# The last query group in two parts, a seventh buffer of exponentials, clears on VectorE, and a later planned use of the broadcast reciprocals, in a fused attention and feed-forward kernel

## The chip, the cores and the metric

One Trainium2 chip (trn2), one core. The metric is the device time of one execution in microseconds; smaller is better. The **span** of a profile runs from the first to the last instruction and is some 1.7 us shorter. PE is TensorE, DVE is VectorE, ACT is ScalarE, POOL is GpSimd, SP is the queue that issues transfers.

## The reference, cut

```python
def reference(A_x, A_wqkv, A_wo, B_x, B_w1, B_w2, B_w3, B_w4):   # x: 1 x 2048 x 640, bf16
    def _A_ref(x, wqkv, wo):                                     # 32 heads of 20
        ...
        scores = jnp.einsum("bhqd,bhkd->bhqk", q, k) * (Dh ** -0.5)
        p = _softmax(scores, axis=-1)
        o = jnp.einsum("bhqk,bhkd->bhqd", p, v)
        return (...)(o, 0, 2, 1, 3).reshape(B, S, D) @ wo
    ...                                                          # _B_ref: two feed-forward blocks
    xn = _layernorm(x, axis=-1)
    s = _A_ref(xn, A_wqkv, A_wo)
    g = _silu(_B_ref(xn, B_w1, B_w2, B_w3, B_w4))
    ...                                                          # out = a product of s and g, plus x
```

The heart is 32 x 2048 x 2048 exponentials. Four heads ("a quad") and 512 queries make a **group**; there are 8 x 4 = 32 groups. A group has 16 key tiles of 128, and each key tile needs two exponentials of 128 x 1024 elements.

## The kernel before, the parts that matter

The program is a list of tasks. A planner in the kernel file gives every task a place in the order of its engine, from modelled durations and hand-tuned due times (`DUE`); a change of any number can move everything. The table `ND` says, for every quad and group, how many **units** DVE takes: a unit is one pair of key tiles, of which DVE computes half in place of ACT (by bit arithmetic, two reads of 128 x 1024 and four pieces), so a unit takes two exponentials off ACT.

```python
        self.POOLN = [1, 9, 13, 15]          # normalisations done by POOL
        self.ND = (
            [1, 2, 3, 3],                    # quad 0, its four groups
            ...
            [4, 3, 1, 2])                    # quad 7
...
            pl.pool("PT", 6)                 # buffers of exponentials
...
        T("pool", 3000, lambda e: e.memset(self.QM[:, :, :, :], 0.0), ..., name="qm0")
        T("pool", 1500, lambda e: e.memset(self.KT[:, 1, :], 0.0), ..., name="kt0")
        T("pool", 1500, lambda e: e.memset(self.QT[:, 1, :], 0.0), ..., name="qt0")
...
    # end of a group: sums to DRAM and back, reciprocals, broadcast by DMA, product
        T("sp", C_SP, lambda e: e.dma_start(RB[:, :], bass.AP(dr.tensor, ...)), ..., name=f"r1{quad}_{qc}", dlat=1100.0)
        T("dve", c_dve(512, "1x"), lambda e: e.tensor_tensor(dst, Ob[:, :], RB[:, :], op=ALU.mult),
          reads=[A("Ob"), A("RB")], writes=[dsta], name=f"on{quad}_{qc}")
...
    # last quad, after a group: output projection, gate, sum, store, for each of its 4 results
            else:
                for hh in range(2):
                    self.wo_mult("wob", n, hh, range(cfg.KC + 1), SB2[:, sl, :], A("SB2", sl, hh))
            T("dve", c_dve(cfg.D, "2x"), lambda e, ...: e.tensor_tensor(OS[:, sl, :], SB2[:, sl, :], addend, op=ALU.add), ..., name=f"cmb{n}")
            T("sp", C_SP, lambda e, sl=sl, n=n: e.dma_start(outv[:, n, :], OS[:, sl, :]), ...)
```

`wob` is the projection of attention's result (PE, twelve tasks of four matmuls of 320 columns per result); its eviction on DVE multiplies by the gate. There are 16 results of 128 rows; the last four can only be finished after the last exponential.

Of the kernel before, what the change touches and what calls it, by code (L numbers as in the profile page):

```python
# [610 lines left out]
class Cfg:  # L611
# [5 lines left out]
    def __init__(self, S=2048, D=640, H=32, F=1536):  # L617
        self.S, self.D, self.H, self.F = S, D, H, F
        self.DH = D // H
        assert self.DH == 20 and D % 128 == 0 and F % 128 == 0 and S % 512 == 0  # L620
        self.NT = S // 128
        self.NQC = S // 512
        self.KC = D // 128
        self.FC = F // 128
        self.NQUAD = H // 4
        self.QW = 4 * self.DH
        self.scale = self.DH ** -0.5
        self.OFFSET = 60.0
        self.T0 = 38000.0
        self.STEP = 960.0  # L630
        self.DUE = dict(
            k0=100.3, k1=-164.3, k2=-87.4, k3=-108.7, k4=-66.2, v0=-24.5, v0s=-0.38, v1=48.3, v1s=-24.33, w1=675.4,
            w1s=6.41, g1=135.1, x1=243.0, x1s=-5.42, wo=135.2, st=56.8, g3_0=400.7, g3_2=603.1, si_0=451.5, si_2=689.9,
            sis=9.71, u0=9.1, s0=-19.7, u1=5.8, s1=19.9, u2=-21.8, s2=-19.6, u3=-17.5, s3=-7.9, u4=-6.0, s4=-6.6,
            u5=-24.2, s5=8.6, u6=-28.0, s6=-9.3, u7=-1.9, s7=126.8)
        self.BLK = [(2, 3), (6, 7), (10, 11), (14, 15)]
        self.RESERVE = 1000.0
        self.POOLN = [1, 9, 13, 15]
        self.HPE = 0.0
        self.HDVE = 0.0  # L640
        self.THIRD = False
        self.FALL = True
        self.SAVE = 1
        self.AHEAD = 3
        self.UNITS = ((),
                      ((3, 0, 1),),
                      ((0, 0, 2), (2, 1, 2)),
                      ((0, 0, 2), (2, 1, 2), (7, 0, 1)),
                      ((0, 0, 2), (1, 1, 2), (3, 0, 2), (5, 1, 2)))
        self.HPS = 6  # L650
        self.FILL = 0
        self.ROWK = [[], [], [], [], []]
        self.ND = (
            [1, 2, 3, 3],
            [3, 3, 3, 4],
            [3, 3, 3, 3],
            [2, 3, 4, 4],
            [4, 2, 2, 4],
            [4, 3, 3, 3],
            [4, 4, 2, 3],  # L660
            [4, 3, 1, 2])

    def order(self, quad, qc):



        nb = self.ND[quad][qc]
        used = [k for b in self.BLK[:nb] for k in b]
        ks = [k for k in range(self.NT) if k not in used]
        at = {}  # L670
        for j, (pos, r, n) in enumerate(self.UNITS[nb]):
            at.setdefault(pos, []).append(("b", j, r, n))
        out = []
        for i in range(len(ks) + 1):
            out += at.pop(i, [])
            if i < len(ks):
                out.append(("k", ks[i], i in self.ROWK[nb]))
        assert not at
        return out
# [37 lines left out]
class Gen:  # L717
# [71 lines left out]
    def build(self, plan_only=False):  # L789
        nc, pl = self.nc, self.pl  # L790
        with contextlib.ExitStack() as es:
# [21 lines left out]
            pl.pool("PT", 6)  # L813
# [51 lines left out]
    def setup_consts(self):  # L865
# [34 lines left out]
        self.maskn6 = m6  # L900
        Mm = self.Mm = self.alloc("Mm", [2, 32], BF16)
        T("pool", 200, lambda e: e.memset(Mm[:, :, :], 0.0), writes=[A("Mm", 0), A("Mm", 1)], name="Mm0")

    def alloc_persistent(self):
# [19 lines left out]
        self.PT = self.alloc("PT", [6, 1024], BF16)  # L924
        self.QM = self.alloc("QM", [2, 4, 512], BF16)
        T("pool", 3000, lambda e: e.memset(self.QM[:, :, :, :], 0.0), writes=[A("QM", k) for k in range(2)], name="qm0")
# [23 lines left out]
        T("pool", 1500, lambda e: e.memset(self.KT[:, 1, :], 0.0), writes=[A("KT0")], name="kt0")  # L950
        T("pool", 1500, lambda e: e.memset(self.QT[:, 1, :], 0.0), writes=[A("QT0")], name="qt0")
# [16 lines left out]
    def ln_tiles(self, tag, tiles, dst_of, dst_atoms_of, ve_out=None):  # L968
# [27 lines left out]
        for li, n in enumerate(tiles):  # L996
            pool = ve_out and n in cfg.POOLN
            T("pool" if pool else "dve", 160 + 0.86 * D if pool else c_dve(D, "4x"),
# [5 lines left out]
    def ln_tiles_act(self, tag, tiles):  # L1004
# [10 lines left out]
        for li, n in enumerate(tiles):  # L1015
            T("act", c_act(D) + 135, lambda e, li=li, n=n: e.activation(J[:, :], xn[:, n, :], AF.Copy, accum_out=sv[:, 0, li:li + 1]),
              reads=[A("xn", n)], writes=[A(tag + "_J"), A(tag + "_sv", 0, li)], name=f"{tag}_sx{n}")
            T("act", c_act(D) + 135, lambda e, li=li, n=n: e.activation(J[:, :], xn[:, n, :], AF.Square, accum_out=sv[:, 1, li:li + 1]),
              reads=[A("xn", n)], writes=[A(tag + "_J"), A(tag + "_sv", 1, li)], name=f"{tag}_sxx{n}")
# [14 lines left out]
        for li, n in enumerate(tiles):  # L1034
            if n in self.cfg.POOLN:
                T("pool", 160 + 0.86 * D,
# [3 lines left out]
            T("act", c_act(D) + 40,  # L1040
# [25 lines left out]
    def ln1_and_transpose(self):  # L1066
# [5 lines left out]
        for g0 in range(0, NT, 8):  # L1072
            for k0, L in ((0, 2), (2, 2), (4, 1)):
                tl = list(range(g0 + k0, g0 + k0 + L))
                tmp += self.ln_tiles(f"ln1_{g0 + k0}", tl, lambda n: xn[:, n, :], lambda n: [A("xn", n)], ve_out=True)
            tmp += self.ln_tiles_act(f"ln1a_{g0}", list(range(g0 + 5, g0 + 8)))
        self.ln1_tmp = tmp
        bk = 0
        for g in range(4):
            for kc in range(cfg.KC):  # L1080
                b = bk % 4
                act = bk % 2 == 1
# [187 lines left out]
    def v_proj(self, hf):  # L1270
# [8 lines left out]
        T("pool", c_pool(cfg.NT * 16), lambda e: e.memset(VA[:, :, :, :, 20:21], 1.0), writes=allv, name=f"VA1_{hf}")  # L1279
        T("pool", c_pool(cfg.NT * 16), lambda e: e.memset(VA[:, :, :, :, 21:22], 0.0), writes=allv, name=f"VA0_{hf}")  # L1280
# [18 lines left out]
    def attn_quad(self, quad):  # L1299
# [9 lines left out]
        for qc in range(NQC):  # L1309
# [3 lines left out]
            if col:  # L1313
# [3 lines left out]
                  stream="qm", ndma=4)  # L1317
            done, total = [0], sum(5 if x[0] == "b" else 1 for x in seq)
# [3 lines left out]
            for kind, x, *unit in seq:  # L1322
                if kind == "k":
                    if col and unit[0]:
                        heads = (0, 2, 1, 3)
                        slots = [self.score_half(b, qc, x, a, gb) for a in range(2)]
                    else:
                        heads = range(4)
                        slots = [self.score_act(b, qc, x, a, gb if col else None) for a in range(2)]
                    kts = (x, x)  # L1330
                else:
# [4 lines left out]
                    heads = range(4)  # L1336
# [4 lines left out]
                def fnpv(e, kts=kts, slots=slots, ends=ends, heads=heads):  # L1341
                    pb = self.bank(PVB)
                    first, final = ends()
                    for x, i in enumerate(heads):
                        ins = e.matmul(pb[32 * i:32 * i + 22, 0:512], VA[:, ql, kts[x // 2], i, :],  # L1345
                                       PT[:, slots[x // 2][0].slot, 512 * (x % 2):512 * (x % 2) + 512],
# [5 lines left out]
            if last:  # L1352
                self.finish_qc(qc)
                if qc == 0:
                    self.part_qc(NQC - 1)

# [33 lines left out]

    def score_half(self, b, qc, kt, a, gb):

        T, A = self.T, self.A
        hs, sa = self.stile()
        def fn(e):
            for jj in range(2):
                r = slice(64 * jj, 64 * jj + 64)
                ins = e.matmul(self.bank(hs.slot + jj)[:, :], self.KT[r, b, 128 * kt:128 * kt + 128], self.QM[r, gb, a + 2 * jj, :],
                               start=True, stop=True, tile_position=(64 * jj, 0))
            return ins  # L1400
        T("pe", 220, fn, reads=self.turns() + [("gate",), A("KT", b, kt // 4), A("QM", gb)],
          writes=[sa, ("turn", self.step)], name=f"sc{self.step}", mode=1, cls=-1, acq=("S", hs))
        return self.exp_act(hs, sa)
# [74 lines left out]
    def normalise(self, quad, qc):  # L1478
# [7 lines left out]
        if last:  # L1486
            dst, dsta = self.On7[:, 512 * qc:512 * qc + 512], A("On7", qc)
        else:
            dst, dsta = self.On[:, ob, :], A("On", ob)
        if last:  # L1490
            OnT = self.On[:, ob, :]
            cls = -2 if qc == cfg.NQC - 1 else -1
# [10 lines left out]
            T("dve", c_dve(512, "1x"), lambda e: e.transpose(dst, OnT[:, :]), reads=[A("On", ob)], writes=[dsta], name=f"on{quad}_{qc}", cls=cls)  # L1503
# [14 lines left out]
          reads=[("dr", ob)], writes=[A("RB")], is_dma=True, nbytes=128 * 2048, name=f"r1{quad}_{qc}", stream="r1", dlat=1100.0)  # L1518
        T("dve", c_dve(512, "1x"), lambda e: e.tensor_tensor(dst, Ob[:, :], RB[:, :], op=ALU.mult),  # L1519
          reads=[A("Ob"), A("RB")], writes=[dsta], name=f"on{quad}_{qc}")  # L1520
# [7 lines left out]
    def load_wo(self):  # L1528
# [7 lines left out]
        T("pool", 1500, lambda e: e.memset(OTq[:, :, KC - 1, :], 0.0), writes=[A("OTq", k) for k in range(2)], name="otq0")  # L1536
        self.Sb = self.alloc("Sb", [4, D], BF16)
# [10 lines left out]
    def wo_tile(self, name, n, hh, parts, dst_atoms, first_reads=()):  # L1548
# [13 lines left out]
        def rd(k):  # L1562
            return [A("OTq", o), A("Wo")] if ps[k] < KC else [A("On7", n // 4), A("Wo7")]
# [29 lines left out]
    def wo_last(self, n, dst, dsta):  # L1593
# [11 lines left out]
        T("pe", c_pe(8, HALF), fn, reads=[A("On7", n // 4), A("Wo7")], writes=[sa], name=f"wob{n}", acq=("S", hs))  # L1605
# [22 lines left out]
    def finish_qc(self, qc):  # L1628
# [8 lines left out]
        for nl in range(4):  # L1637
# [9 lines left out]
            else:  # L1647
                for hh in range(2):
                    self.wo_mult("wob", n, hh, range(cfg.KC + 1), SB2[:, sl, :], A("SB2", sl, hh))
            T("dve", c_dve(cfg.D, "2x"), lambda e, sl=sl, addend=addend: e.tensor_tensor(OS[:, sl, :], SB2[:, sl, :], addend, op=ALU.add),  # L1650
              reads=adda + [A("SB2", sl, 0), A("SB2", sl, 1)], writes=[A("OS", sl)], name=f"cmb{n}")
            T("sp", C_SP, lambda e, sl=sl, n=n: e.dma_start(outv[:, n, :], OS[:, sl, :]),
              reads=[A("OS", sl)], writes=[("out", n)], is_dma=True, nbytes=128 * cfg.D * 2, name=f"st_out{n}", stream=f"out{sl}",
# [18 lines left out]
    def b_alloc1(self):  # L1672
# [9 lines left out]
        vea = [A("VE", n) for g0 in (0, 8) for n in (g0, g0 + 2, g0 + 4, g0 + 5)]  # L1682
# [19 lines left out]
        self.RR = self.alloc("RR", [7, 512], FP32)  # L1702
# [8 lines left out]
    def b_w1(self):  # L1711
# [6 lines left out]
        for ch in range(cfg.NQC):  # L1718
            for m in range(KC):
                r = (KC * ch + m) % 7  # L1720
# [146 lines left out]
```

## Time and profile before

The time is best read as four terms: the **head** up to the first exponential, ACT's **work** from there to the end of the last exponential, ACT's **idle** time in that stretch, and the **tail** after it. They sum to the span of the profiled run.

| term, us | before |
|---|---|
| head | 35.65 |
| ACT work | 823.3 |
| ACT idle | 14.1 |
| tail | 11.05 |
| span of the profiled run | 884.1 |
| median time | 886.55 (885.6 to 886.58, 3 runs) |

The lines of the profile that carry these are in the prediction below.

### The profile page before, as it was taken

The numbers are of one execution on the slowest core, as the hardware profiler recorded it, in microseconds if no ns is written. First come the engines' busy times: TensorE is split into PE (matmuls) and PEld (weight loads), VectorE is DVE, ScalarE is ACT, GpSimd is POOL, SyncE is SP. The second block draws the span as 40 slices with busy tenths as digits, with TensorE's granted clock in tenths as the row PEclk, the third lists the DMA queues.
The fourth block names the chain that finished last, engine by engine and source line by source line (L and its number), as shares of the span: only waits on it lengthen the run. The fifth ranks groups of instructions, "written<-read, shape, count | busy, mean of one in ns | idle before, by whom it ended". The sixth has DMA issues, their size and how long they took to land.

```text
span 884.1 us, 34138 instructions
## 1 busy us (share of the span) xinstructions
PE 822.8 (93%) x15594; PEld 361.9 (41%) x15594; DVE 716.2 (81%) x986; ACT 846.9 (96%) x896; POOL 42.9 (5%) x74
## 2 busy tenths in 40 slices
PE   3899999998999999999999899999999799999996
PEld 2433333333444443433334444443433344444553
DVE  7747797876888889999998657997889794898675
ACT  7799999998999999999999999999999999999994
POOL 9500000000000000000000000000000000010000
PEclk9999999999999999999999999999999999999998
DMA  6002632331210002332122302132221212023322
GB/s 224 10 8 61 137 96 73 95 95 36 52 41 25 26 25 64 90 101 52 47 55 62 113 26 56 54 91 69 56 64 44 70 32 69 24 65 101 114 69 75
DMA packets 86481, 59.01 MB, mean 67 GB/s; under 512 B 53057, under 2 KB 77841, under 8 KB 86337
## 3 DMA queue, kind: packets, MB, share of 16 engines
q1 hardware_dynamic: 86336, 56.82, 23.5%
q8 instruction: 123, 2.02, 0.9%
q14 instruction: 22, 0.17, 0.1%
HBM read 42.10 MB, written 10.63 MB: 60 GB/s over the span
## 4 chain that ended last, share of the span: by engine, by line
ACT 55%; PE 19%; DVE 17%; DMA 5%; POOL 1%; issue 1%; POOLq 0%
ACT arena L1444 53%; PE psum L782 8%; PE psum L1420 6%; DVE arena L1371 5%; DVE arena L1471 4%; DMA arena<-recips 3%; PE psum L1345 2%; PE psum L1388 2%; DMA recips<-arena 2%; PE psum L1380 1%; ACT arena L1809 1%; DVE arena L984 1%; ACT arena L1825 1%; DVE arena L1805 1%; DVE arena L1225 1%
## 5 line engine op out<-in xcount | busy, mean ns | idle before, releaser
L1444 ACT ACTIVATE arena<-psum 128x1024 bf16<-128x1024 f32 x834 | 777.8, 1038 | 14.4 <-PE psum L1420 5.0
L1420 PE MATMUL psum<-arena 128*32 128x512 bf16 x4928 | 375.7, 381 | 8.0 <-ACT arena L1444 6.6
L782 PE MATMUL psum<-arena 128*32 128x320 bf16 (+1 forms) x5952 | 359.8, 333 | 6.8 <-DVE arena L1179 2.8
L1471 DVE TENSOR_SCALAR arena<-psum 128x1024 uint16<-128x1024 f32 (+1 forms) x192 | 231.5, 1206 | 42.1 <-PE psum L1388 41.3
L1371 DVE TENSOR_SCALAR arena<-arena 128x4096 uint16<-128x4096 uint16 (+1 forms) x224 | 231.4, 1059 | 3.6 <-PE psum L1380 2.5
L782 PEld LDWEIGHTS psum<-arena 128*32 128x32 bf16 x5952 | 150.5, 97 | 146.2 <-issue 20.7
L1345 PE MATMUL psum<-arena 128*22 128x512 bf16 x1668 | 161.8, 381 | 1.2 <-DVE arena L1506 0.6
L1420 PEld LDWEIGHTS psum<-arena 128*32 128x32 bf16 x4928 | 104.4, 95 | 137.2 <-ACT arena L1444 95.2
L1380 PE MATMUL psum<-arena 128*22 128x512 bf16 x1520 | 126.5, 380 | 2.5 <-DVE arena L1371 2.2
L1388 PE MATMUL psum<-arena 32*128 32x512 bf16 x816 | 85.4, 384 | 16.6 <-ACT arena L1444 9.7
L1345 PEld LDWEIGHTS psum<-arena 128*22 128x22 bf16 x1668 | 42.5, 92 | 55.8 <-issue 11.8
L1388 PEld LDWEIGHTS psum<-arena 32*128 32x128 bf16 x816 | 21.9, 90 | 102.5 <-ACT arena L1444 81.4
L1380 PEld LDWEIGHTS psum<-arena 128*22 128x22 bf16 x1520 | 35.8, 91 | 44.5 <-issue 9.7
L1805 DVE CAST arena<-psum 128x512 bf16<-128x512 f32 x48 | 32.8, 684 | 8.3 <-PE psum L782 8.1
L1225 DVE CAST arena<-psum 128x512 bf16<-128x512 f32 x40 | 27.3, 682 | 10.9 <-PE psum L782 10.8
L1820 DVE TENSOR_TENSOR arena<-psum,arena 128x320 bf16<-128x320 f32 x32 | 15.6, 486 | 22.0 <-PE psum L782 22.0
L1590 DVE SCALAR_TENSOR_TENSOR arena<-psum,arena 128x320 bf16<-128x320 f32 x32 | 15.6, 489 | 19.0 <-PE psum L782 18.9
L1519 DVE TENSOR_TENSOR arena<-arena 128x512 bf16<-128x512 f32 x28 | 19.2, 686 | 11.5 <-DMA arena<-recips 11.4
L984 DVE BATCH_NORM_STATS2 arena<-arena 128x6 f32<-128x320 bf16 x52 | 23.0, 480 | 2.2 <-DMA arena<-in_A_x_dram 2.2
L1286 DVE CAST arena<-psum 128x320 bf16<-128x320 f32 x32 | 15.4, 488 | 10.9 <-PE psum L782 10.5
L1506 DVE COPY arena<-psum 128x512 f32<-128x512 f32 x28 | 19.2, 685 | 3.5 <-PE psum L1345 2.3
L1089 PE MATMUL psum<-arena 128*32 128x128 bf16 x320 | 8.9, 248 | 13.7 <-DVE arena L999 13.1
(103 smaller groups left out, 283.8 us busy)
## 6 DMA issues: line engine op xcount, KB each, us to landing
arena<-in_B_w_dram SPq DMA_DIRECT2D x48, 160.0 KB, 2.6
arena<-recips SPq DMA_DIRECT2D x28, 256.0 KB
arena<-arena SPq DMA_DIRECT2D x124, 32.0 KB, 1.9
arena<-in_B_w_dram SPq DMA_DIRECT2D x4, 960.0 KB, 6.0
arena<-in_A_x_dram SPq DMA_DIRECT2D x8, 320.0 KB, 5.3
arena<-in_A_x_dram SPq DMA_DIRECT2D x16, 160.0 KB, 2.3
out_dram<-arena SPq DMA_DIRECT2D x16, 160.0 KB, 1.8
heads<-arena SPq DMA_DIRECT2D x112, 20.0 KB
```

Source lines behind the costliest of these rows:

```text
L782: ins = e.matmul(pb[32 * c:32 * c + 32, 0:N], lhsT(k, c), rhs(k, c), start=(k == 0), stop=(stop and k == nk - 1), tile_position=(0, 32 * c))
L984: lambda e, li=li, n=n, hh=hh: e.bn_stats(st[:, li, 6 * hh:6 * hh + 6], xn[:, n, hD * hh:hD * hh + hD]),
L1225: T("dve", c_dve(512), lambda e, h=h, c=c: e.tensor_copy(KS[:, 512 * c:512 * c + 512], self.wbank(h)[:, 0:512]), reads=[wa], writes=[A("KS ...
L1345: ins = e.matmul(pb[32 * i:32 * i + 22, 0:512], VA[:, ql, kts[x // 2], i, :], PT[:, slots[x // 2][0].slot, 512 * (x % 2):512 * (x % 2) + 512],
L1371: T("dve", c_dve(w, "4x"), lambda e, v=v, dst=dst: e.tensor_scalar(dst, U[:, ub, 0:w], 0.5, EXP_B[v], op0=ALU.mult, op1=ALU.add), reads=ha ...
L1380: ins = e.matmul(pb[32 * i:32 * i + 22, 0:512], wv, dst[:, at:at + 512].bitcast(BF16), start=first, stop=final, tile_position=(0, 32 * i))
L1388: return e.matmul(out, self.KT[32 * i:32 * i + 32, b, 128 * kt:128 * kt + 128], self.QT[32 * i:32 * i + 32, b, 512 * qc:512 * qc + 512], s ...
L1420: ins = e.matmul(out[32 * c:32 * c + 32, :], self.KT[:, b, 128 * kt + 32 * c:128 * kt + 32 * c + 32], self.QM[:, gb, 2 * a + jj, :], start ...
L1444: lambda e: e.activation(self.PT[:, hp.slot, :], self.psum[:, 512 * hs.slot:512 * hs.slot + 1024], AF.Exp, scale=cfg.scale),
L1471: ins = e.tensor_scalar(U[:, ub, 1024 * at + 512 * k:1024 * at + 512 * k + w], self.psum[:, 512 * hd.slots[k]:512 * hd.slots[k] + w], a_ex ...
L1506: T("dve", c_dve(512), lambda e: e.tensor_copy(Ob[:, :], self.bank(self.PVB)[:, :]), writes=[("PV", 0), A("Ob")], name=f"ob{quad}_{qc}", c ...
L1805: T("dve", c_dve(512), lambda e, h=h, fc=fc, i=i: e.tensor_copy(GT[:, i, fc, :], self.wbank(h)[:, 0:512]), reads=[wa], writes=at, name=f"g ...
```

## The change

Its intent, as far as the code shows it: take more exponentials off ACT, end sooner by letting the first half of the last 512 queries be finished beside the second, keep ACT supplied through one more buffer, free GpSimd of three clears, and let the planner know that the broadcast of the reciprocals lands later than it assumed. Besides, all due times and several modelled costs were set anew, so the order of the whole program is another one.

```diff
-            k0=100.3, k1=-164.3, ..., s7=126.8)
+            k0=164.5, k1=-174.5, ..., s7=52.2)                 # all due times
-        self.POOLN = [1, 9, 13, 15]
+        self.POOLN = [6, 7, 9, 12, 14]
+        self.LNA = [3, 4]                                       # LayerNorm tiles on ACT, of 8 and 8
+        self.TRA = [9, 11, 15, 19]                              # transposed evictions on ACT: 4, not 10
+        self.LAST = [[[4, 2], [7, 1]], [[6, 1]]]                # units in the two halves of the last group
-            [4, 3, 1, 2])
+            [4, 4, 3, 0])                                       # and other rows of ND
-            pl.pool("PT", 6)
+            pl.pool("PT", 7)
-        T("pool", 3000, lambda e: e.memset(self.QM[:, :, :, :], 0.0), ..., name="qm0")
+        T("dve", c_dve(4096, "4x"), lambda e: e.memset(self.QM[:, :, :, :], 0.0), ..., name="qm0", due=-40000.0)
         # the same for KT ("kt0") and QT ("qt0")
-            T("act", c_act(D) + 135, ...   # LayerNorm sums on ACT
+            T("act", c_act(D) + 260, ...   # and other modelled costs, nearer to the measured ones
+            if last and qc == NQC - 1:
+                for half in range(2):
+                    self.last_half(quad, qc, half, gb)           # scores, exponentials, products of 256 queries
+                self.finish_qc(qc)
-          ... name=f"r1{quad}_{qc}", stream="r1", dlat=1100.0)
+          ... name=f"r1{quad}_{qc}", stream="r1", dlat=3600.0)
-        self.RR = self.alloc("RR", [7, 512], FP32)              # pays for the seventh buffer
+        self.RR = self.alloc("RR", [6, 512], FP32)
```

## The prediction

> **What bounds the kernel now.** I read the page first: its busy shares, then its chain of work, then the group of exponentials.
>
> ```profile
> span 884.1 us, 34138 instructions
> PE 822.8 (93%) x15594; PEld 361.9 (41%) x15594; DVE 716.2 (81%) x986; ACT 846.9 (96%) x896; POOL 42.9 (5%) x74
> ACT 55%; PE 19%; DVE 17%; DMA 5%; POOL 1%; issue 1%; POOLq 0%
> L1444 ACT ACTIVATE arena<-psum 128x1024 bf16<-128x1024 f32 x834 | 777.8, 1038 | 14.4 <-PE psum L1420 5.0
> ```
>
> ACT (ScalarE) is the fullest engine and its exponentials are over half of the chain. One lasts 1038 ns, but 834 of them cover only 777.8 us, so they overlap and one more costs 777.8 / 834 = 0.933 us. That is the price I use. PE's 93% is close, but each separate group of matmuls carries a modelled end (four of 512 columns show 0.39 us and follow each other in 0.22), so it has more room than it shows.
>
> Next I cut the span where the first exponential starts and the last one ends, and asked for each engine's busy time in the three stretches:
>
> ```profile
> core 0: us, PE busy (x) PEld busy (x) DVE busy (x) ACT busy (x) POOL busy (x), PEclk, DMA share, GB/s
> 0.00:35.65 35.65, 20.01 (x592) 12.83 (x596) 28.07 (x86) 23.61 (x46) 30.37 (x50) 1.00 0.46 145
> 35.65:873.05 837.40, 800.29 (x14962) 348.22 (x14957) 680.51 (x889) 823.32 (x851) 12.55 (x24) 1.00 0.24 63
> 873.05:884.10 11.05, 2.54 (x52) 0.80 (x44) 7.62 (x13) 0.01 (x1) 0.00 (x0) 0.78 0.22 76
> ```
>
> So the span is head 35.65 + ACT work 823.3 + ACT idle 14.1 + tail 11.05 us. Each part of the change acts on one of these four terms. DVE (VectorE) off ACT's path is free until it delays PE.
>
> The idle is not spread evenly. The timeline has its largest piece at 207 us:
>
> ```profile
> 207.21 0.69 DVE L1519 TENSOR_TENSOR arena<-arena 128x512 bf16<-128x512 f32 x1 [2.86 <-DMA arena<-recips]
> 209.18 0.40 PE L1388 MATMUL psum<-arena 32*128 32x512 bf16 x4 [2.43 <-DVE arena L1471]
> 209.62 1.02 ACT L1444 ACTIVATE arena<-psum 128x1024 bf16<-128x1024 f32 x1 [2.18 <-PE psum L1388]
> ```
>
> and the stretches just after it, in the same columns as above:
>
> ```profile
> 209.50:212.00 2.50, 2.50 (x36) 1.10 (x36) 2.46 (x4) 1.80 (x2) 0.00 (x0) 0.64 0.05 13
> 212.00:214.00 2.00, 2.00 (x28) 0.77 (x20) 0.18 (x1) 1.27 (x2) 0.00 (x0) 0.59 0.00 0
> ```
>
> Read the brackets downwards: DVE stands 2.86 us at the broadcast reciprocals, PE then 2.43 us at a DVE eviction, ACT 2.18 us at PE. In the two stretches PE's granted clock (third number from the end) is 0.64 and 0.59, and ACT loses another 1.5 us in short gaps before 215 us. Up to 224 us the gaps come to some 4.5 us, from one early-placed DVE instruction.
>
> In the head I looked for small DVE operations with long durations:
>
> ```profile
> 31.69 2.15 POOL L951 MEMSET arena<- 128x2048 bf16 x1
> 31.72 2.15 DVE L1166 TENSOR_SCALAR arena<-arena 128x4 bf16<-128x4 f32 x1
> ```
>
> L1166 has four elements per partition, yet lasts exactly as long as POOL's clear beside it. A similar one (L992, two elements) is 0.98 us long under POOL's 3.51 us clear of 4096 elements; others of its kind take 0.15. L1166 is on the path to the first exponential: PE waits 1.7 us for it.
>
> **What the Trainium skill says.** (1) "SBUF — State Buffer", section "Who interferes with whom": a DVE instruction in a two-port mode and GpSimd share a port pair, and whoever issues first blocks the other entirely. The trace agrees (2.15 beside 2.15 us). (2) "VectorE: DVE Perf Modes", section "Zero memsets can be issued as uint32 (trn2)": a memset takes one cycle per element whatever the type, so a zero fill of bf16 costs half if issued as 4-byte words. This speaks against the planner's own charge for the new DVE clears, which is a quarter of a cycle. The trace before has one DVE clear only, 512 f32 elements of PSUM in 0.485 us, one per cycle. (3) "TensorE: Matmul & The Clock Gate", Part 1: too little activity throttles the PE clock, and it needs some microseconds of work to return. The trace agrees (0.64 and 0.59 for about 4 us). (4) "ScalarE: Activation LUTs", section "What ACT_TABLE_LOAD costs": 186 ns + 0.833 per element, back-to-back overlap about 93 ns; an estimate from it is 1039 ns long and 946 apart. Here 1038 and 933; I use the measured 933.
>
> **The change part by part.**
>
> Exponentials. The table of DVE blocks sums to 95 before and 96 after, the last group now having none in it, but four 1024-wide units of its own (three in its first half, one in the second). One block takes two exponentials from ACT. Before: 32 groups x 32 - 2 x 95 = 834, which is the row's count. After: 31 x 32 - 2 x 96 + (32 - 4) = 828. That is 6 x 0.933 = **-5.6 us** of ACT work. DVE gets more: four units replace the four tiles of two blocks in the last group, and elsewhere there are 96 - 93 = 3 blocks more, each two reads of 1.22 us plus four pieces of some 0.6 us (1.22 for two blocks), 4.9 us; together 15 us, or under 2% of its time. PE gets slightly less.
>
> Tail. Now, after the last exponential: last products, transpose 0.72, reciprocal 0.25, product 0.69, transpose 0.71, matmul 0.5, then four pairs of products and sums (0.78 + 0.44 each), then the store, 2.2 us from the last DVE end to the end: 11.05. After, 256 columns and two tiles remain. From DVE rows of 320 and 512 elements (0.487 and 0.685 us) an element costs 1.03 ns, so each of the three 512-wide steps drops 0.26; the reciprocal perhaps 0.05; two pairs drop out, 2 x 1.22 = 2.44; a last set of wide products in pieces leaves, 0.5. Sum 0.79 + 0.05 + 2.44 + 0.5 = **-3.8 us**. The first half's finish, about 4.1 us of DVE, lies beside the second half's exponentials (15 x 0.933 = 14 us).
>
> Head. Three clears leave POOL: 3.51 + 1.80 + 2.15 = 7.5 us. They stop blocking L1166 (-2.0 us on the path), L992 (0.8), and two small ones at 16.2 us that are 0.9 long (0.8). DVE gets 8192 elements: as 4-byte words 4096 / 0.96 GHz = 4.3 us, an estimate from the skill's page; it stands idle for 2.2 us before the first x lands, so some 2.1 us delay its statistics. Six transposed evictions move from ACT to DVE (+6 x 0.42 = 2.5), one tile's statistics leave it (-1.1), and one slow POOL normalisation of 2.5 us goes. DVE thus gains and loses nearly alike; the path loses mainly L1166, and ACT is relieved: **-2.0 us**.
>
> Idle. The plan now allows 2.5 us more for the broadcast to land. The issue before the long stall was at 201.66 and the use at 207.21, 5.5 us; nine such stalls (11.4 us of DVE) mostly vanish, and with them the 4.5 us at 207. The seventh buffer answers ACT's waits on the value products (4.8 us in 6 waits), but these come with late DVE evictions (0.9 us of PE at 451), which stay possible. A new plan has new stalls of its own. I take 14.1 to 9: **-5 us**.
>
> Sum: -5.6 - 3.8 - 2.0 - 5 = -16.4, that is 870.2 from 886.55. I add 0.8 for the last group, where PE does two fewer of its cheap row-tiled score blocks (0.33 us per key tile against 2 x 0.43): **871.0 us**.
>
> **Rivals.**
> (A) The clears cost DVE more than they free. If they run as bf16, 8.5 us, the statistics start at 10 us instead of 3.7 and the head grows by some 4 us in place of losing 2. For it: DVE is busy for 28 of the first 35.65 us and goes first into the clears. Against: the word form halves it. The time would be about 877.
> (B) A new plan, new idle. PE, 93% busy, or DVE with 15 us more to do starts to hold ACT up; the removed fallback for score buffers leaves fewer places. For it: DVE is at 93% between 300 and 500 us already. Against: ACT idles under 5 us in that stretch. With idle still 14 the time is 876, with 18, 880.
> (C) The re-planned order does better. The layer norms now end at 26.7 us, behind late small DVE steps; with costs nearer to the measured ones the first exponential could start at 31.5, and idle fall to 6. The time would be about 866.
> (D) The tail is hidden anyway: it can't be, for nothing runs beside it on ACT after 873.05.
>
> **Range and chances.** Exponentials and tail, -9.4 us, follow from counts and I trust them to 1 us. Head and idle are each uncertain by 3 to 4 us, which together is about 5: range 865 to 878. Faster by over 2% means below some 869, a third of a standard deviation and more below my value: 0.34. Slower by 2% would need 27 us of new idle over my estimate: 0.02. The rest, 0.64, is within 2%.
>
> **What would show each step.** Right: 828 exponentials at 0.933 us; last exponential to end about 7.3 us, with two pairs on DVE in it; first exponential at 33 to 34 us, L1166 near 0.15 us; DVE clears of about 2.1 and 1.1 us; waits on the reciprocals under 3 us; ACT idle near 9. Wrong: DVE clears of 4.3 us and a head above 36; ACT idle over 14, waiting for PE behind DVE evictions; or a tail where half 0's finish still holds DVE when the last products come.

## The result, and the profile after

The changed kernel took **882.61 us** (median of 4 runs, 881.24 to 884.17) beside 886.37 of the kernel before on the same chip (4 runs, 885.6 to 886.58). The ratio of the fast runs is 0.996, with a 95% interval of 0.9938 to 0.9982: a real gain of 0.4%, and within 2% "the same". The prediction was 871.0 with a range of 865 to 878; the result lies outside it. Ratios here are the mean time of one kernel's runs over the mean of the other's of the same rounds, so not quite the ratio of the medians quoted.

The page of the changed kernel, for the counts that the prediction named:

```profile
span 882.5 us, 34883 instructions
...
PE 827.6 (94%) x15958; PEld 370.6 (42%) x15958; DVE 730.4 (83%) x1005; ACT 838.6 (95%) x887; POOL 36.1 (4%) x71
...
L1526 ACT ACTIVATE arena<-psum 128x1024 bf16<-128x1024 f32 x828 | 771.7, 1038 | 11.0 <-PE psum L1390 3.3
...
L1601 DVE TENSOR_TENSOR arena<-arena 128x512 bf16<-128x512 f32 x28 | 19.1, 683 | 3.1 <-DMA arena<-recips 3.1
```

There are 828 exponentials, 771.7 / 828 = 0.932 us each: counted right. The product with the reciprocals (L1601) waits 3.1 us in place of 11.4.

The three stretches of the changed kernel, in the columns of the prediction (time, PE, PE weights, DVE, ACT, POOL, PE's granted clock, DMA share, GB/s):

```profile
0.00:40.69 40.69, 25.63 (x720) 16.41 (x724) 34.33 (x98) 21.43 (x42) 23.59 (x50) 1.00 0.43 127
40.69:868.39 827.70, 795.77 (x15090) 349.49 (x15090) 686.14 (x886) 817.20 (x845) 12.52 (x21) 1.00 0.24 63
868.39:882.50 14.11, 6.17 (x160) 4.68 (x150) 9.96 (x22) 0.00 (x1) 0.00 (x0) 0.78 0.32 106
```

Head 40.69; work 817.20; idle 827.70 - 817.20 = 10.5; tail 14.11. Against before: **+5.0, -6.1, -3.6, +3.1**, sum -1.6 for these two profiled runs (medians: -3.8). The two terms in the middle came near the prediction, the two ends went the other way. A second profile of the same kernel (below) gives +5.4, -7.0, -5.5, +3.0.

**The head.** DVE's timeline, each line with start, duration, engine, line, operation, and in brackets the idle time before it with its releaser:

```profile
1.30 1.76 DVE L930 MEMSET arena<- 128x2048 uint32 x1 [1.30 <-PEq L1939]
3.22 0.91 DVE L954 MEMSET arena<- 128x1024 uint32 x1 [0.16 <-issue]
...
5.72 1.16 DVE L956 TENSOR_SCALAR arena<-arena 128x2048 bf16<-128x2048 bf16 x1
6.81 3.23 DVE L988 BATCH_NORM_STATS2 arena<-arena 128x6 f32<-128x320 bf16 x8
...
38.56 0.24 DVE L1171 TENSOR_SCALAR arena<-arena 128x4 bf16<-128x4 f32 x1
```

The clears run as 4-byte words, as the prediction supposed, and take DVE from 1.3 to 5.2 us (1.76 and 0.91 us each, a little less than the 2.1 and 1.1 predicted); the addition on KT, the keys, follows, and the first LayerNorm statistics start at 6.81 us (3.68 before). The small step that GpSimd's clear had held for 2.15 us now takes 0.24 (L1171). And ACT in the same stretch:

```profile
6.17 0.74 ACT L1020 ACTIVATE arena<-arena 128x640 bf16<-128x640 bf16 x1 [4.09 <-DMA arena<-in_A_x_dram]
...
20.95 0.92 ACT L1045 ACTIVATE arena<-arena 128x640 bf16<-128x640 bf16 x1 [5.78 <-DVE arena L1036]
...
30.62 0.92 ACT L1045 ACTIVATE arena<-arena 128x640 bf16<-128x640 bf16 x1 [4.32 <-DVE arena L1036]
```

ACT, which was to be relieved, waits for its first tile of x until 6.17 us (3.68 before; the loads stand in another order, with the 400 KB of value weights fifth among them), and twice for a tiny DVE step (L1036), 5.78 and 4.32 us, which stands in DVE's order behind other work. DVE has 34.33 us of work in the head in place of 28.07, PE 25.63 in place of 20.01: twelve value tiles are evicted there and not seven, and a second conversion of queries has moved in.

**The tail.** The timeline after the end of the last exponential at 868.39 us:

```profile
868.67 3.47 PE L785 MATMUL psum<-arena 128*32 128x320 bf16 x96
...
872.47 0.54 PE L1380 MATMUL psum<-arena 128*22 128x256 bf16 x12
...
873.32 0.42 DVE L1426 TENSOR_SCALAR arena<-arena 128x1024 uint16<-128x1024 uint16 x1
...
873.79 0.29 PE L1380 MATMUL psum<-arena 128*22 128x256 bf16 x4 [0.78 <-DVE arena L1426]
874.46 0.45 DVE L1441 STREAM_TRANSPOSE arena<-psum 128x256 f32<-128x256 f32 x1
...
879.25 0.89 DVE L1737 TENSOR_TENSOR arena<-arena 128x640 bf16<-128x640 bf16 x2
```

For 3.5 us PE works through 96 matmuls of output projections (L785) that belong to the group before the last. Only then come the last unit's value products (L1380, 872.47), the last of them waits for a DVE piece (L1426) that is itself late, and the transpose that starts the finish of the second half (L1441) begins at 874.46, six microseconds after the last exponential. DVE works 9.96 us in this tail, 7.62 before.

### The profile page after: what moved, and what is told of

Its sections match the earlier page's. It is cut to its first block, busy times and chain, and to the rows that moved or that the text cites. A ratio compares the mean times of both kernels' runs of the same rounds, so it can differ in the third digit from the quotient of the medians.

```text
span 882.5 us, 34883 instructions
## 1 busy us (share of the span) xinstructions
PE 827.6 (94%) x15958; PEld 370.6 (42%) x15958; DVE 730.4 (83%) x1005; ACT 838.6 (95%) x887; POOL 36.1 (4%) x71
## 4 chain that ended last, share of the span: by engine, by line
ACT 66%; PE 25%; DVE 6%; DMA 2%; issue 1%; SPq 0%; DVEq 0%
ACT arena L1526 62%; PE psum L785 10%; PE psum L1502 7%; ACT arena L1896 2%; PE psum L1349 2%; PE psum L1484 2%; PE psum L1390 2%; PE psum L1476 2%; DMA queries<-arena 1%; ACT arena L1912 1%; DVE arena L1553 1%; DVE arena L1467 1%; DVE arena L988 1%; PE psum L1380 0%; DVE arena L1104 0%
## 5 line engine op out<-in xcount | busy, mean ns | idle before, releaser
L1526 ACT ACTIVATE arena<-psum 128x1024 bf16<-128x1024 f32 x828 | 771.7, 1038 | 11.0 <-PE psum L1390 3.3
L1502 PE MATMUL psum<-arena 128*32 128x512 bf16 x4640 | 353.2, 381 | 10.3 <-ACT arena L1526 8.5
L785 PE MATMUL psum<-arena 128*32 128x320 bf16 (+1 forms) x5952 | 356.7, 335 | 4.9 <-DVE arena L1291 1.6
L1553 DVE TENSOR_SCALAR arena<-psum 128x1024 uint16<-128x1024 f32 (+1 forms) x194 | 234.3, 1209 | 46.3 <-PE psum L1484 45.8
L785 PEld LDWEIGHTS psum<-arena 128*32 128x32 bf16 x5952 | 149.7, 97 | 135.2 <-issue 24.7
L1502 PEld LDWEIGHTS psum<-arena 128*32 128x32 bf16 x4640 | 97.6, 95 | 138.8 <-ACT arena L1526 104.2
L1349 PE MATMUL psum<-arena 128*22 128x512 bf16 x1600 | 152.3, 381 | 0.8 <-DVE arena L1588 0.4
L1476 PE MATMUL psum<-arena 128*22 128x512 bf16 x1536 | 124.5, 380 | 1.0 <-DVE arena L1467 0.9
L1907 DVE TENSOR_TENSOR arena<-psum,arena 128x320 bf16<-128x320 f32 x32 | 15.6, 487 | 12.2 <-PE psum L785 11.9
L1676 DVE SCALAR_TENSOR_TENSOR arena<-psum,arena 128x320 bf16<-128x320 f32 x32 | 15.6, 487 | 10.2 <-PE psum L785 10.2
L1821 DVE TENSOR_TENSOR arena<-psum,arena 128x512 bf16<-128x512 f32 x20 | 13.8, 688 | 10.6 <-PE psum L785 10.6
L1094 PE MATMUL psum<-arena 128*32 128x128 bf16 x320 | 8.6, 245 | 14.2 <-DVE arena L1003 12.8
L1601 DVE TENSOR_TENSOR arena<-arena 128x512 bf16<-128x512 f32 x28 | 19.1, 683 | 3.1 <-DMA arena<-recips 3.1
```

Source lines behind the costliest of these rows:

```text
L785: ins = e.matmul(pb[32 * c:32 * c + 32, 0:N], lhsT(k, c), rhs(k, c), start=(k == 0), stop=(stop and k == nk - 1), tile_position=(0, 32 * c))
L1349: ins = e.matmul(pb[32 * i:32 * i + 22, 0:512], VA[:, ql, kts[i // 2], i, :], PT[:, slots[i // 2][0].slot, 512 * (i % 2):512 * (i % 2) + 512],
L1476: ins = e.matmul(pb[32 * i:32 * i + 22, 0:512], wv, dst[:, at:at + 512].bitcast(BF16), start=first, stop=final, tile_position=(0, 32 * i))
L1502: ins = e.matmul(out[32 * c:32 * c + 32, :], self.KT[:, b, 128 * kt + 32 * c:128 * kt + 32 * c + 32], self.QM[:, gb, 2 * a + jj, :], start ...
L1526: lambda e: e.activation(self.PT[:, hp.slot, :], self.psum[:, 512 * hs.slot:512 * hs.slot + 1024], AF.Exp, scale=cfg.scale),
L1553: ins = e.tensor_scalar(U[:, ub, 1024 * at + 512 * k:1024 * at + 512 * k + w], self.psum[:, 512 * hd.slots[k]:512 * hd.slots[k] + w], a_ex ...
```

## The experiments

Twelve kernels ran, four each on one chip with its own runs of the kernel before (medians 886.37, 886.39 and 886.69 us), each with five timed rounds. Where an edit moves single tasks, the planner first plans as always; then the order of every engine is edited at the named places and planned a second time with the orders held fixed. The traces bear this out: in h_late and b_clears every engine's order is that of the kernel edited, but for the moved tasks. t_light and t_unsplit are of another kind: they change numbers of the plan and are planned anew, and by their traces the order of VectorE and PE is the changed kernel's up to some 799 and 835 us and another one after that. The kernels c_light, c_unsplit and c_pool rest on such plans too. Terms of all runs, us, from one profile each:

| kernel | head | ACT work | ACT idle | tail | span | median | ratio to before |
|---|---|---|---|---|---|---|---|
| before | 35.65 | 823.3 | 14.1 | 11.05 | 884.1 | 886.37 | 1 |
| a_again (the change) | 41.09 | 816.3 | 8.6 | 14.09 | 880.1 | 883.24 | 0.9965 |
| h_late | 38.27 | 817.1 | 12.3 | 13.77 | 881.4 | 882.28 | 0.9947 |
| t_light | 41.17 | 821.3 | 8.6 | 8.74 | 879.8 | 882.29 | 0.9953 |
| b_on | 36.44 | 822.4 | 10.7 | 11.05 | 880.5 | 883.56 | 0.9967 |
| b_clears | 35.66 | 823.0 | 15.0 | 11.04 | 884.7 | 885.94 | 0.9994 |
| t_unsplit | 40.49 | 816.2 | 7.8 | 16.85 | 881.3 | 882.05 | 0.9948 |
| c_light | 38.30 | 821.3 | 8.5 | 8.72 | 876.9 | 879.31 | 0.9921 |
| c_unsplit | 39.15 | 819.4 | 6.7 | 10.83 | 876.0 | 878.24 | 0.9914 |
| h_v9 | 37.43 | 817.5 | 15.0 | 14.10 | 884.0 | 885.22 | 0.9986 |
| b_pt7 | 35.87 | 822.9 | 15.3 | 11.12 | 885.2 | 886.26 | 0.9989 |
| t_pool | 41.76 | 816.3 | 10.3 | 15.32 | 883.7 | 885.81 | 0.9992 |
| c_pool | 38.16 | 820.1 | 8.4 | 10.74 | 877.4 | 878.73 | 0.9909 |

The 95% intervals are about 0.0017 either way in the first call and 0.0016 to 0.0024 in the others, so 1.5 to 2 us; differences between two rows under that are read from the terms, if at all. Idle varies by 2 us between two profiles of one kernel (10.5 and 8.6 for the change); head and tail are steadier, though the head of b_on, in which nothing was edited, is 0.8 us longer than that of the kernel before.

### The changed kernel again

No edit.

> The changed kernel unaltered, so that the experiments beside it have it on the same chip: 0.994 to 0.998 of the kernel before (some 881 to 884 us), first exponential at about 40.7 us, tail about 14 us.

It came so: 0.9965 (0.9948 to 0.9982), head 41.09, tail 14.09.

### h_late: the clears behind the start of attention

```diff
+        move("dve", ["qm0"], after="s0_0_0_3")
+        move("dve", ["kt0", "kt1", "qt0"], after="qev_2")
```

> The changed kernel with its three clears and the addition on KT moved on VectorE behind the start of attention, all other orders kept. Theory A (the clears at the front of VectorE's order delay the LayerNorm, and that delays the first exponential): the first exponential comes at 36.5 to 38 us instead of 40.7, and the time falls by 2.5 to 4 us against the changed kernel. Theory B (the head is long because of the work packed into it: twelve evictions of V and a second query conversion ahead of the first exponential): the first exponential moves by less than 1 us and the time by less than 1 us.

```profile
0.00:38.27 38.27, 25.56 (x720) 16.27 (x724) 30.04 (x94) 21.46 (x42) 23.56 (x50) 1.00 0.45 135
```

The head is 38.27 in place of 41.09 us (DVE's work in it 30.04 in place of 34.4). Over all profiles with early clears in the new plan the head is 40.5 to 41.8, over the four with late clears alone as the head's edit 38.2 to 39.2: some 2.5 us are those of the clears and of the addition on KT, which was moved with them (means 41.0 and 38.5). That is just short of what theory A said (36.5 to 38), and half of the five us lost. The other half (38.3 against 35.65) is something else. The time fell by 0.0018 of the kernel before, 1.6 us and not the 2.5 to 4 of theory A, which by itself is at the limit of what five rounds show; the pair t_light and c_light below differ by 0.0032 with the same edit. They were run at other times.

### b_clears: the clears early on VectorE, in the kernel before

```diff
+        for n, d, spot in (("qm0", 1140.0, "pv0"), ("kt0", 600.0, "qm0"), ("qt0", 600.0, "kt0")):
+            ...                                   # from POOL's order to the front of DVE's
+            t.eng, t.dur = "dve", d
```

> The kernel before with its three clears moved from GpSimd to the front of VectorE's order, where the changed kernel has them, all other orders kept. Theory A (the switch of engine is what lengthened the head): the first exponential comes 3 to 5 us later than in the kernel before (from 35.7 to 36.4 us to 39 to 41) and the time rises by 2 to 5 us. Theory B (what VectorE loses at its front GpSimd's earlier power steps give back, as the prediction had it): the first exponential moves by less than 1 us or comes earlier, and the time stays within 1 us.

Theory A fell here: the first exponential starts at 35.66 us, and the time is the same (0.9994, 0.9978 to 1.0011). Its DVE timeline shows why:

```profile
5.71 0.82 DVE L1024 BATCH_NORM_STATS2 arena<-arena 128x6 f32<-128x320 bf16 x2
...
33.60 0.24 DVE L1206 TENSOR_SCALAR arena<-arena 128x4 bf16<-128x4 f32 x1
```

The statistics start 2.0 us later than before (5.71, not 3.68), and the last key eviction on ACT 1.9 us later (33.41, not 31.53); then the small step which a GpSimd clear held for 2.15 us in the kernel before takes 0.24, and the 1.9 us are back. That is the sum that the prediction made (2.1 us lost at DVE's front, 2.0 gained at L1166), and in this plan it is right. So the switch of engine alone costs nothing in the old plan. In the new plan the same early clears, there with the addition on KT, cost 2.5 us. That the new order gives them no such return, as both they and GpSimd's hold can be avoided there, is likely but was not tested by itself.

### h_v9: the late value tiles back behind the first exponentials

```diff
         # besides the two moves of h_late
+        first = 9
+        for n in range(first, 16):
+            move("pe", [f"v0_{n}_{k}" for k in range(5)], after=steps[2 * (n - first) + 1])
+            ...                                   # and their evictions on DVE likewise; two tasks on GpSimd later
```

> The changed kernel with the clears late and, besides, the value projections from tile 9 on (products and evictions) moved behind the first exponentials, nearer to where the kernel before has them. Theory A (the packed-in work is the rest of the longer head, but has to be done somewhere): first exponential 0.5 to 1.5 us earlier than with late clears alone (37 to 37.8 us), ScalarE's idle time between 40 and 70 us up by 1 to 3 us, the time the same as with late clears alone or up to 2 us more. Theory B (it was packed in needlessly): the first exponential comes earlier and no idle time is added, 1 us or more off the time.

The stretch from 40 to 70 us, first of h_late, then of this kernel:

```profile
40.00:70.00 30.00, 28.68 (x350) 7.79 (x338) 17.79 (x23) 28.90 (x32) 1.05 (x2) 0.94 0.07 15
```

```profile
40.00:70.00 30.00, 28.79 (x390) 9.35 (x388) 16.52 (x24) 25.55 (x28) 1.35 (x4) 0.92 0.07 16
```

The first exponential came 0.84 us earlier (37.43), and between 40 and 70 us ACT works 25.55 us in place of 28.90: 3.35 us given back, more than the 1 to 3 expected. Theory A holds for the two terms, and the time is worse by more than the 2 us that it allowed, 0.9986 against 0.9947 (some 3.5 us). What the new plan packs into the head is not waste; it saves more idle time later than it costs, with these orders at least. The rest of the longer head (LayerNorm steps late in DVE's order, x loaded in another order) was not taken apart further.

### t_light: less for VectorE at the end

```diff
-            [4, 4, 3, 0])
+            [4, 3, 2, 0])
-        self.LAST = [[[4, 2], [7, 1]], [[6, 1]]]
+        self.LAST = [[[4, 2]], []]
```

> The changed kernel with less for VectorE in the last set of heads: 4, 3, 2 units instead of 4, 4, 3, and one unit of two tiles in the first half of the last group instead of three units; 834 exponentials instead of 828. Theory A (VectorE is full there, so each exponential taken off ScalarE near the end comes back in the tail): the last exponential ends some 4 us later, the tail shrinks from 14.1 to 9 to 10.5 us, and the time stays within 1.5 us of the changed kernel. Theory B (the tail is long because of the order in which PE takes the projections and the last products, not because of VectorE's load): the tail stays at 13 to 14 us and the time rises by 4 to 5 us.

Six more exponentials make ACT's work 5.05 us longer than in a_again (821.34 to 816.29), and the tail is 5.35 us shorter (8.74 to 14.09). The time is the same within the interval. With 834 exponentials the count is that of the kernel before, so the six that the change took off ACT all lie in the last quad, and they bought nothing that this run can show: what ACT gave, the tail took.

Theory A's figures came. Is its reason, a full VectorE, the right one? VectorE is fuller after the change, as 800 to 830 us show, before, after and in this run (fourth number, the DVE time, in 30 us; the second lines, from 830 us, are for t_unsplit below):

```profile
800.00:830.00 30.00, 29.52 (x620) 15.12 (x624) 23.98 (x37) 29.34 (x32) 0.00 (x0) 1.00 0.30 92
830.00:860.00 30.00, 29.91 (x660) 15.50 (x652) 20.49 (x34) 29.64 (x33) 0.00 (x0) 1.00 0.27 86
```

```profile
800.00:830.00 30.00, 29.50 (x596) 13.48 (x592) 29.67 (x40) 29.66 (x34) 0.00 (x0) 1.00 0.25 76
830.00:860.00 30.00, 30.00 (x908) 21.95 (x904) 23.49 (x41) 26.47 (x29) 0.00 (x0) 1.00 0.26 77
```

```profile
800.00:830.00 30.00, 30.00 (x652) 15.36 (x648) 26.48 (x41) 29.03 (x33) 0.00 (x0) 1.00 0.28 81
```

But PE is full in all of them. From 800 us to the end of the last product with the values, for a_again, this run, t_unsplit and the kernel before:

```profile
800.00:871.69 71.69, 70.79 (x1876) 46.72 (x1876) 60.97 (x101) 62.09 (x67) 0.00 (x0) 1.00 0.26 78
800.00:871.40 71.40, 70.67 (x1868) 45.38 (x1860) 48.84 (x83) 68.00 (x74) 0.00 (x0) 1.00 0.26 79
800.00:871.01 71.01, 70.13 (x1492) 35.22 (x1492) 60.68 (x89) 64.11 (x70) 0.00 (x0) 1.00 0.27 80
800.00:873.95 73.95, 73.38 (x1576) 37.94 (x1576) 51.00 (x82) 72.03 (x78) 0.00 (x0) 1.00 0.27 84
```

PE stands still for 0.6 to 0.9 us of each stretch. The last product ends at 871.69, 871.40 and 871.01 us in the three new runs, although the last exponential ends at 866.01, 871.06 and 864.45. So in the last 70 us PE's work sets when the last product comes, and an ACT that is done sooner waits for it in the tail. VectorE has 61.0 us of work in this stretch of a_again and 48.8 in this run, and the last product comes at the same time; all that PE waits for VectorE there is 0.78 us, before the very last product (the L1426 shown above). VectorE's load is thus not what made the tail long, but for that 0.78 us. How much another order on PE could bring was not tested: this run is planned anew from 799 us on, PE's order included.

### t_pool: additions on GpSimd, meant to relieve VectorE alone

```diff
+        for n in range(0, 12):
+            t = ts[ix("cmb%d" % n)]
+            o["dve"].remove(t.id)
+            t.eng, t.dur = "pool", 1500.0
+            o["pool"].append(t.id)
```

> The changed kernel with twelve of the last sixteen additions (results 0 to 11) moved from VectorE to GpSimd, which does nothing there: 5.9 us of VectorE's work less in the last 90 us. Theory A (VectorE's load sets the end): the tail falls from 14.1 to 11.5 to 12.5 us and the time by 1.5 to 2.5 us. Theory B (PE's order sets it): tail and time within 0.7 us. A third way: GpSimd's additions take so long (over 2 us) that the stores behind them end later than before, and the time rises.

It came nearest to the third way, though the additions do not take over 2 us: 0.9992 (0.9973 to 1.0011), tail 15.32 us. Two lines of the timeline in the tail:

```profile
873.59 1.39 POOL L1776 TENSOR_TENSOR arena<-arena 128x640 bf16<-128x640 bf16 x1 [1.09 <-DMA arena<-in_A_x_dram]
873.82 1.44 DVE L1465 TENSOR_SCALAR arena<-arena 128x1024 uint16<-128x1024 uint16 x1
```

An addition that takes DVE 0.49 us takes GpSimd 1.4. Worse, the DVE piece that the last products wait for (L1465, 1024 elements) lasts 1.44 us and ends just after GpSimd's addition, where the same instruction took 0.42 in the changed kernel. This is the lock on the shared ports that the Trainium skill describes in "SBUF — State Buffer", section "Who interferes with whom", and the trace agrees with it. PE, too, waits once for a GpSimd addition (0.34 us, at 870.8). So this run by itself says nothing on whether DVE's load set the tail.

### t_unsplit: the last group undivided

```diff
-            if last and qc == NQC - 1:
+            if False:
-            [4, 4, 3, 0])
+            [4, 4, 3, 2])
-            cls = -1
+            cls = -2 if qc == cfg.NQC - 1 else -1
```

> The changed kernel with the last group of queries in one part of 512 again, with two units on VectorE in it, 828 exponentials as before; the plan is the same up to some 830 us. Theory A (the end is set by VectorE's and PE's leftover projections, so halving the last products takes nothing off it): the last exponential ends some 4 us earlier, the tail is 17 to 19 us, the time within 1.5 us of the changed kernel. Theory B (halving saves what was predicted, 3.8 us, and something else spoiled the tail): the time is 3 to 4 us above the changed kernel's.

0.9948 (0.9929 to 0.9967), not above the change's 0.9965: theory A, though the last exponential ends only 1.6 us earlier than in a_again (864.45 to 866.01), not 4. The division does shorten the tail (14.1 instead of 16.85): from the end of the last product to the end of the program it is 8.4 us in a_again and 10.3 here. But ACT waits more before it; the stretch from 830 to 860 us without the division:

```profile
830.00:860.00 30.00, 29.62 (x636) 14.91 (x632) 23.85 (x36) 30.00 (x34) 0.00 (x0) 1.00 0.25 72
```

ACT is busy for all 30.00 us; in the changed kernel for 26.47 (shown above; 26.42 in a_again). There it waits three times, 3.3 us in all, for scores of the halves (L1390). (In the totals of the table this shows as 0.8 us only, 8.6 to 7.8, because idle time earlier in the program varies.) The halves take twice as many score matmuls per exponential (908 matmuls in 30 us, not 636), but each is half as wide: 16 of 256 columns take PE 0.44 us (861.94 to 862.38 us in the changed kernel), 8 of 512 columns 0.43 in the kernel before. So the count as such is not the cause; why these scores come late on a full PE was not taken apart. The prediction had 0.8 us for the last group's scores.

### b_on: nothing but later use of the reciprocals, in the kernel before

```diff
+        for j, s in {0: 1, 2: 2, 5: 3, 6: 2, 8: 1, 9: 3, 11: 2, 16: 5, 25: 1}.items():
+            ...                     # the j-th product with the reciprocals goes s places back in DVE's order
```

> The kernel before with nothing changed but VectorE's order at nine places: each multiplication by the broadcast reciprocals that waited for its transfer stands one to five instructions later. Theory A (these waits pass on to PE and ScalarE, as at 207 us): the waits for the reciprocals fall from 11.4 us to under 3, ScalarE's idle time between first and last exponential from 14.1 to some 10 to 11 us, and the time by 3 to 4 us, that is, as much as the whole change gained. Theory B (most of that waiting is slack, or another wait takes its place): ScalarE's idle time falls by less than 1.5 us and the time by less than 1.5 us.

Theory A held, with a time just short of its 3 to 4 us. The waits for reciprocals fell to 3.0 us (two of them), ACT's idle time to 10.7, and the time to 0.9967 (0.9951 to 0.9982). The timeline where the kernel before stalled at 207 us now has one unbroken run of twelve exponentials:

```profile
202.12 11.39 ACT L1487 ACTIVATE arena<-psum 128x1024 bf16<-128x1024 f32 x12
```

Nine DVE instructions, moved by one to five places, gain 2.8 us of median, as much as the whole change within the error (0.9965).

### b_pt7: a seventh buffer, in the kernel before

```diff
-            pl.pool("PT", 6)        # in the second planning only; the order stays
+            pl.pool("PT", 7)
-        self.PT = self.alloc("PT", [6, 1024], BF16)
+        self.PT = self.alloc("PT", [7, 1024], BF16)
```

> The kernel before with a seventh buffer of exponentials and nothing else: every engine's order is kept, room comes from freeing two small tiles early. If buffers of exponentials hold ScalarE up: its idle time of 14.1 us falls by 1 us or more and the time by 1 us or more. If not (no wait on a free buffer shows in ScalarE's waits): within 0.7 us of the kernel before.

0.9989 (0.9968 to 1.001), ACT's idle 15.3 in place of 14.1: no gain of idle time, and none of the time that this run can show. With the order held, the buffer as such isn't what ACT waits for. What a plan made for seven buffers gains from them is left open.

### c_light and c_unsplit: the edits together

c_light is h_late and t_light in one. c_unsplit has the late clears and, without the division, `[4, 3, 3, 1]` in the last row: 832 exponentials.

> The changed kernel with both edits: the clears behind the start of attention and the lighter load on VectorE in the last set of heads. If the two gains add up: first exponential at 38 to 38.5 us, tail 8.5 to 9.5 us, and 2 to 3 us less than the changed kernel (0.993 of the kernel before). If the head's gain is given back by later waits: the same as the lighter load alone, 0.995.

> The changed kernel with the clears late and the last group undivided, with 4, 3, 3, 1 units in the last set of heads: 832 exponentials. If the division brings nothing: 2 to 3 us under the changed kernel, tail 11 to 13 us. If the division is worth something: 1 us or more above the combination that keeps it.

c_light came to 0.9921 (0.9904 to 0.9938), head 38.30, tail 8.72: each end as in the single edit, and the time, 3.9 us under the change, falls by more than the 2 to 3 expected. c_unsplit is 878.24 us, 0.9914 (0.9895 to 0.9933), **8.2 us under the kernel before and 4.4 under the change** (882.61), and the simpler program. Its second stretch:

```profile
39.15:865.17 826.02, 795.29 (x14826) 342.52 (x14822) 683.50 (x882) 819.37 (x849) 12.53 (x21) 1.00 0.24 64
```

Read against c_light, this is the division at its best, with no backlog in front of it: its tail is 8.72 us, without it 10.83, so it takes some 2.1 us off. It has 8.5 us of idle time against 826.02 - 819.37 = 6.65, and two exponentials more. The two differ in their units as well, so 2.1 is an estimate; between the times, 0.9921 and 0.9914, nothing can be told.

### c_pool: the additions on GpSimd, in the lighter plan

The same edit as t_pool on c_unsplit.

> The undivided combination (late clears, 4, 3, 3, 1 units) with the same twelve additions on GpSimd. If VectorE still sets the end: 1 to 2 us under that combination (876 to 877.5 us). If the lighter load already removed that: the same within 0.7 us.

0.9909 (0.9889 to 0.9928), tail 10.74: the same as c_unsplit. Taking more off VectorE in this way brings nothing in the lighter plan.

## Why the prediction was wrong

By its own steps, in us:

| step | predicted | measured (first profile; second) | verdict |
|---|---|---|---|
| exponentials | -5.6 | -6.1; -7.0 | right |
| idle, with the last group's scores | -5 + 0.8 | -3.6; -5.5 | right in sum |
| head | -2.0 | +5.0; +5.4 | failed |
| tail | -3.8 | +3.1; +3.0 | failed |
| sum | -15.6 | -1.6; -4.0 | 11.8 off in medians |

**The exponentials** were counted right, and their price of 0.933 us held. But "each part of the change acts on one of these four terms" was too simple: the six fewer lie in the last quad, and there ACT's work and the tail are one sum (t_light). What the count gave, the tail took back.

**The tail.** Two steps failed. One is that PE "has more room than it shows". In the last 74 us it had none even before the change (busy for 73.38 of 73.95 us), so ending the exponentials sooner there did not bring the last product sooner (a_again and t_light): between the two ends lie 0.9 us before the change and 5.7 after it. That is the 3.5 us of older projections and what follows them.

The other is "After, 256 columns and two tiles remain". It sized what follows the last product: 3.8 us less. Measured from the end of that product it is 8.4 us with the division (8.36 in a_again, 8.35 in t_light) and 10.2 to 10.3 without (the kernel before, t_unsplit), so 1.8 to 2.0 less. Part of what is missing is the sign named under "Wrong", half 0's finish, which wasn't given any weight in the sum: in t_light, with no backlog, one of its products and two of its sums (0.79, 0.44 and 0.48 us of DVE) still stand between the two transposes of the second half. And the division costs 3.3 us of waiting from 830 to 860 us (t_unsplit), not 0.8.

**The head.** The failed step is "DVE thus gains and loses nearly alike". The balance for clears against L1166 was right, as b_clears shows in the old plan. It left out what the re-set due times and costs move into the head: five more value evictions, a query conversion, another order of the loads. DVE's work there rose by 6.3 us. Of the 5 us, 2.5 are the early clears in the new plan, with the addition on KT (h_late); the rest goes with the new order, and the part of it that could be tried (h_v9) pays for itself later. Over the whole program DVE got 14.2 us more (716.2 to 730.4), near the 15 predicted, though 15 is 2.1% of its time and not "under 2%". Rival A had the right sign (877, head +4), though half of its size has another cause, and its condition, clears as bf16, wasn't met.

**The idle time** fell for the reason given: late use of the reciprocals, alone worth 2.8 us (b_on). The seventh buffer, on which some of the 5 us rested, showed nothing by itself (b_pt7). Rival B (new idle from PE) was right for the last group, hidden in a sum that came out; that the sum came out is in part luck.

So the change gained some 10 to 12 us in the middle and lost 8 at the ends, where the 6 us of fewer exponentials went as well.

## What to carry to other kernels

When work is taken off the engine that bounds the whole, ask in each stretch which engine is full there: ACT bounds most of this kernel, but PE was full in its last 74 us, and exponentials taken off ACT in them came back as tail. In a tail, queued work counts and not only the chain of the last item. A change that also re-plans everything should be taken apart with the orders held fixed: here nine instructions moved by a few places gave as much as the whole change, and its best-looking part, the division of the last group, could be left out at no cost that the runs show. A cost that is free in one order (clears hidden behind a step that was held anyway) is not free in another.

## What the Trainium skill lacked or had wrong

- "Trainium Architecture — The Big Picture", section "The five engines, in one table": it gives GpSimd as 2x slower than DVE for streaming elementwise work. Here an addition of two 128x640 bf16 tiles took 1.40 us on GpSimd and 0.49 on VectorE, 2.9 times as long.
- "ScalarE: Activation LUTs", section "What ACT_TABLE_LOAD costs": its overlap of about 93 ns gives an estimate of 946 ns from one 1024-wide exponential to the next; the runs show 932 to 933 ns over 828 and 834 of them. The difference, 1.4%, is 11 us of this span.
- "VectorE: DVE Perf Modes", section "Zero memsets can be issued as uint32 (trn2)": one cycle per element, at the 0.96 GHz that the page gives, would be 1.04 ns a word. The runs show 1.76 us for a clear of 2048 words and 0.91 for 1024, so 0.83 ns for each word more, a fifth less.
